# A fused attention and two-MLP kernel: 64-row transposes made with 128 rows, x sums on VectorE, g loaded first, and new plan offsets

## The chip, the cores and the metric

The program runs on one core of a Trainium2 chip. Its time is the device time of one execution in microseconds. Five engines work side by side from their own queues, each in program order: TensorE (PE, with its weight loads as PEld), VectorE (DVE), ScalarE (ACT), GpSimd (POOL) and SyncE (SP), which here issues all loads and stores.

## What is computed

In float32, with 4 batches, 12 heads, 448 tokens and a head size of 64:

```python
q_n, k_n = rmsnorm(q, g_q), rmsnorm(k, g_k)
scores = q_n @ k_n.T / 8            # per batch and head
attn = exp(scores - max); attn = attn / (sum + 1e-9)
x = concat_heads(attn @ v)          # 1792 x 768
x = ((x @ w_a) * (x @ w_b)) @ w_out         # inner width 1536
h = x @ w_in                                # inner width 2048
return (h * clip(h + 3, 0, 6) / 6) @ moe2_w_out
```

## The kernel before

**Precision.** Most products run as fp32r matmuls. An operand is split into a high half, rounded to fp32r, and a low half, the difference; a product is then three matmuls: high by high, high by low, low by high (`tri`, L694 to L696). Scores take two (L529, L530), with q split alone. Transposes of probabilities and the value product run in plain fp32.

**Tiling.** x lives transposed: six row tiles (m) of 128 features by 448 tokens for each batch. The first group is batches 0 and 1, the second batches 2 and 3. Attention goes head pair by head pair (`pair`, 24 of them). A pair has 896 tokens in seven chunks of 128, of which the fourth holds 64 rows of each head. `turn_k` transposes K for each head on TensorE (four transposes into one PSUM bank, L494). For the first head the fourth of them takes only the lower 64 rows of its chunk. After the scores come row maximum (L535), exponential (L539) and the transposes of the probabilities: `turn_p` for three full column blocks (L568), `turn_rest` for the last 64 columns of each head. `turn_rest` makes four 128x128 transposes (L582), three that give 64x128 (L584) and one of 64x64 rows (L585) that reads only the lower half of the shared chunk. `value` (L600) multiplies by v.

**The MLPs.** The first MLP runs first for batch 0, then batch 1, and the second MLP for both (`layer`), while attention for batches 2 and 3 is done in between. The last part (`layer7`, matmuls at L967) does both MLPs for the second group with a seven-product scheme for 2x2 blocks (as Strassen's). It needs sums and differences of blocks of x. `x_maker` makes them: `minus` (the sums, at `sub`, L393), a ScalarE copy for the high half (L711, L871) and a subtraction for the low half. Its subtractions may run on VectorE or GpSimd. For the first MLP of the second group they are made from `xf`, at the end of `layer(1, ...)`; for the second MLP from `acc`. In `layer7` the sums of weights are at L925, the splits of weights also at L393, and the accumulations of products from PSUM into `acc` or `xf` at L975. The accumulations of `layer` are at L800.

**The order of the work.** One core's queues are filled by a planner (`Plan`). Each operation is added with a due time, and with a cost in nanoseconds for each engine that may run it. `Plan.run` goes through a model of the five engines, and whenever one is free it issues the operation that is ready and due first; a second engine takes an operation if the first is busy and the due time is past by some margin (`LB`, `LF`). The order in which this loop calls the operations is the order of each engine's instructions, fixed for the run. The tables T, TQ, R, OA to OD, LEAD, OW, AFTER, MM, LW7, XLEAD and so on are due offsets, margins and costs of that model. `vg` and `"VG"` say which engines may run a subtraction: V is VectorE, G GpSimd.

**The start.** `gg` is the product of g_q and g_k, from a 1 KB load (L1100); the high half of q is q times gg (L511 on ScalarE, L513 on VectorE), the low half is at L517. The load was due at 0.0, behind the first pair's loads, which are due before 0. The squares for the norms are at L453 (ScalarE) or L455 (VectorE, GpSimd).

Of the kernel before, what the change touches and what calls it, by code (L numbers as in the profile page):

```python
# [18 lines left out]
P = 128  # L19
NB, NH, S, D = 4, 12, 448, 64  # L20
# [7 lines left out]

T = (6.793, 74.014, 253.235, 440.0)
TQ = (1.436, 3.637, 4.788, 4.218)
R = ((85.0, 1.761), (255.0, 1.223), (411.278, 1.34), (703.581, 1.0), (932.169, 1.0))


BS = ((2, 3, 4), (1, 2, 3, 4), (2, 3, 4), (3, 4))
# [7 lines left out]
SQ = ("AG", "A", "A", "A")  # L44
# [10 lines left out]

LB = ((344.344, 276.261, 381.127), (548.658, 402.965, 561.206), (548.658, 402.965, 561.206), (606.623, 311.013, 561.206))
LF = ((548.658, 376.129, 761.141), (548.658, 402.965, 561.206), (548.658, 402.965, 561.206), (553.891, -149.766, 668.974))
LW = 161.162  # L60


OA = (-7.027, -5.631, -5.6, -5.311, -5.026, -4.8, -4.475, -4.381)
OB = (-4.77, -2.7, -3.245, -2.3, -2.091, -2.6, -2.386)
OC = (0.104, -0.677, 0.482, 0.457, 4.632, 4.519)
UT = 5.13
UK = 2.0
OD = (0.4, 1.972, 3.0)


LEAD = 22.604
OW = (-8.493, -9.23, 1.129, 3.002, -1.61)
AFTER = 2.346


SLICE = (3, 3, 2)
# [3 lines left out]

MM = 206.7
LW7 = (26.748, 25.0, 15.217, 11.821)

SLICE7 = ((3, 3), (3, 3, 2))
XLEAD, XSTEP = -11.077, 4.422
LX7 = (10.733, 19.0, 18.5)  # L90


def piece_order(up, down, n, k):
# [214 lines left out]
def on_pool(n):  # L308
    return ((146 + 2.11 * n) * (1.25 if n >= PH else 1.0), True)
# [3 lines left out]
def fused_kernel(ctx: ExitStack, tc: tile.TileContext, nat, qt, gs_in, wpk, outT):  # L313
    nc = tc.nc
    V, A, G, SP = nc.vector, nc.scalar, nc.gpsimd, nc.sync
# [74 lines left out]
    add = plan.add  # L390
# [23 lines left out]
    def pair(n0):  # L414
# [8 lines left out]
        def at(u):  # L423
            return t0 + q * u
# [22 lines left out]
        for i, (lo, hi, who) in enumerate(alike):  # L447
# [3 lines left out]
            def square(e, sl=sl):  # L451
# [3 lines left out]
                    e.tensor_tensor(out=sq.t[:, sl], in0=rn.t[:, sl], in1=rn.t[:, sl], op=ALU.mult)  # L455

            cost = {"V": (on_dve(n), True), "A": on_act(n), "G": on_pool(n)}
            add(at(OA[0]), {k: cost[k] for k in ("VAA"[i] if n0 == 0 else SQ[b])}, square,
                reads=x, writes=sk)
            add(at(OA[1]), {"V": on_dve(n)}, lambda e, sl=sl: e.reduce_sum(out=ms.t[:, sl], in_=sq.t[:, sl], axis=AX.X),  # L460
                reads=sk, writes=m)
# [14 lines left out]
        for i in range(2):  # L476
# [15 lines left out]
            def turn_k(e, i=i, tk=tk):  # L492
                def turn(c, rows, at):
                    e.transpose(tk.t.bitcast(F32R)[:, at:at + rows.stop], kc.t[rows, c].rearrange("p a d -> p (a d)"),  # L494
                                identr[rows, rows])
                everyone = slice(0, P)
                if i == 0:
                    turn(3, lower, 3 * P)
                else:
                    turn(3, everyone, 2 * P + D)  # L500
                for c in range(3):
                    turn(4 * i + c, everyone, c * P)

            add(at(OB[3] + 4 * i), {"PE": 224 + 30 * i}, turn_k, writes=[tk, kks[i]], reads=[
                "identr", *((kc, k, a) for k in range(i + 1) for a in range(2))])
            add(at(OB[4] + 4 * i), {"A": 424}, lambda e, i=i, tk=tk: e.activation(kks[i].t, tk.t[:, :S], AF.Copy),
                reads=[tk], writes=[kks[i]])
# [51 lines left out]
        for k in range(4):  # L559
# [17 lines left out]
            else:  # L577
                t = bank("t", BT[b], False)

                def turn_rest(e, t=t):  # L580
                    for c in range(4):
                        e.transpose(t.t[:, c * P:(c + 1) * P], ps[3 + c].t[:, S - P:], ident)  # L582
                    for c in range(3):
                        e.transpose(t.t[lower, c * P:(c + 1) * P], ps[c].t[:, S - D:], ident)  # L584
                    e.transpose(t.t[lower, 3 * P:S], ps[3].t[lower, S - D:], ident[lower, lower])  # L585

                add(at(u), {"PE": 820}, turn_rest, reads=["ident", *ps], writes=[t, (pt, 0)])
                cost = copy_ps(4 * P)
                add(at(u + OD[0]), {x: cost[x] for x in PT[b]}, lambda e, t=t, pt=pt: copy(
                    e, pt.t[:, :4 * P], t.t), reads=[t], writes=[(pt, 0)])  # L590
# [9 lines left out]
                        e.matmul(pv.t[rows, :S], rv.t[own[i], at_v[i]], pt.t[own[i], cols[i]:cols[i] + S],  # L600
                                 start=k == 0, stop=k == 3)

            add(at(u + OD[1]), {"PE": 1750}, value, reads=[rv, *((t[1], x) for t in pts for x in range(2))], writes=[pv])
            pts = []
        m, due = h // 2, at(u + OD[2])
        if LATE[b]:
# [100 lines left out]
    def split(due, to, src, keys, out, gv, after=()):  # L707

        hi, lo = to
        vg = {"V": (535, True), "G": on_pool(S)}  # L710
        add(due, {"A": 467}, lambda e: e.activation(hi, src, AF.Copy), reads=keys, writes=out[:1], after=after)  # L711
        add(due + 1, {k: vg[k] for k in gv}, lambda e: sub(e, lo, src, f32(hi)),
            reads=[*keys, out[0]], writes=out[1:])
# [115 lines left out]
    def x_maker(src, key, base, after=(), holds=None):  # L829
# [4 lines left out]
        def came(mb, due):  # L834
# [4 lines left out]
            def hold(*those):  # L839
                return [] if holds is None else [holds[n * GB + i] for n, i in those]  # L840

            def at(name):
                return base + XLEAD + XSTEP * ("b11", "t1", "b22", "b21", "t2", "t3", "t4").index(name) + 0.6 * j

            def own(name, m, bi):
                hi, lo = xx[:, m, bi, 0], xx[:, m, bi, 1]
                out = parts(m, bi, ("xh", "xl"))
                split(at(name), (hi, lo), src[:, m, bi], [key(m, bi), *hold((m, bi))], out, "VG")
                sevens[name, j] = (lambda: (hi, lo)), out

            if bi == 0 or m >= HX:
# [2 lines left out]
            if not there.issuperset(all4):  # L854
                return
            (k11, k12, k21, k22), (x11, x12, x21, x22) = zip(*((key(*x), src[:, x[0], x[1]]) for x in all4))
            vg = {"V": (535, True), "G": on_pool(S)}

            def minus(name, out, x, y, reads, writes):
                add(at(name) - 0.5, vg, lambda e: sub(e, out, x, y), reads=reads, writes=writes, after=after)  # L860
# [236 lines left out]

    tails, stored, ends = [], set(), []
    A.preload_act_table_set("natural_log_exp_and_others")
    add(0.0, {"SP": 100}, lambda e: e.dma_start(out=gg, in_=gs_in), writes=["gg"])  # L1100
    add(0.0, {"G": 1500}, lambda e: make_identity(nc, ident), writes=["ident"])
    add(0.1, {"V": 200}, lambda e: e.memset(half_c, 0.5), writes=["half"])
    add(0.1, {"V": 200}, lambda e: e.tensor_copy(identr, ident), reads=["ident"], writes=["identr"])
# [80 lines left out]
```

## Time and profile before

| what | us |
|---|---|
| median of 3 runs | 1257.12 |
| lowest, highest | 1255.7, 1262.59 |
| span of the profiled execution | 1254.4 |
| TensorE busy | 1228.4 |
| VectorE busy | 1031.7 |
| ScalarE busy | 673.3 |
| GpSimd busy | 197.5 |

The time of the profiled execution is one of the runs above; its span, from the first to the last instruction, is 1.3 us below the lowest of them. Busy times are unions of overlapping instructions. Matmuls overlap, so what one costs is read from its start to the start of the next, not from its duration. Idle time is named with what ended it.

### The profile page before, as it was taken

Reading aid. Unit: us, or ns where it says so; the run is one execution under the profiler, and the core shown is the slowest. Engines: PE = TensorE matmul, PEld = TensorE weight load, DVE = VectorE, ACT = ScalarE, POOL = GpSimd, SP = SyncE. Lnnn points to the kernel's source line nnn. Section 1 sums busy time; section 2 is a strip of 40 time slices with the busy share of each in tenths; the row PEclk is TensorE's granted clock in tenths of the full one; section 3 lists DMA queues with packets and bytes.
Section 4 is the critical chain, followed back from the end, with each engine's and each line's share of the span. In section 5 each row is a group of like instructions: output and inputs, shape, how many; then the busy total and the mean of one; then the engine's idle time right before and its main releaser. Section 6 shows DMA issues by size and latency. Waiting matters only on the chain.

```text
span 1254.4 us, 18336 instructions
## 1 busy us (share of the span) xinstructions
PE 1228.4 (98%) x6342; PEld 1046.4 (83%) x6342; DVE 1031.7 (82%) x1906; ACT 673.3 (54%) x1422; POOL 197.5 (16%) x240
## 2 busy tenths in 40 slices
PE   5999999999999999999999999899999999999998
PEld 3678787878988888888788788799999998899998
DVE  7998999997557699888777765796977799988978
ACT  6998776665235545665666664332422245634433
POOL 2433232223011023010121100410000013000000
PEclk9999999999999999999999999899999999999999
DMA  6455766766686587656546442465364544455433
GB/s 203 164 174 186 243 223 228 248 227 230 242 296 241 182 287 272 219 185 227 208 143 207 172 157 77 144 215 161 110 200 143 162 148 129 151 175 165 139 101 126
DMA packets 107853, 235.57 MB, mean 188 GB/s; under 512 B 9200, under 2 KB 74096, under 8 KB 107760
## 3 DMA queue, kind: packets, MB, share of 16 engines
q1 hardware_dynamic: 107760, 234.39, 55.7%
q8 instruction: 50, 0.82, 0.3%
q14 instruction: 43, 0.35, 0.1%
HBM read 162.01 MB, written 72.35 MB: 187 GB/s over the span
## 4 chain that ended last, share of the span: by engine, by line
PE 84%; DVE 9%; DMA 3%; ACT 2%; issue 1%; SPq 0%; DVEq 0%; POOL 0%; ACTq 0%
PE bank L967 30%; PE bank L694 12%; PE bank L696 11%; PE bank L695 11%; PE bank L600 6%; PE bank L568 4%; PE bank L529 3%; PE bank L530 3%; DMA wst<-in_w_dram 2%; PE bank L494 1%; DVE act L393 1%; DVE acc L975 1%; PE bank L582 1%; DVE wf L655 1%; DVE w L393 1%
## 5 line engine op out<-in xcount | busy, mean ns | idle before, releaser
L694 PE MATMUL bank<-xx,w 128*128 128x448 f32 x480 | 184.0, 383 | 1.2 <-ACT p L539 1.1
L696 PE MATMUL bank<-xx,w 128*128 128x448 f32 x480 | 175.7, 366 | 0.0
L695 PE MATMUL bank<-xx,w 128*128 128x448 f32 x480 | 175.5, 366 | 0.0
L967 PE MATMUL bank<-act,w 128*128 128x448 f32 x711 | 153.2, 365 | 0.0
L967 PEld LDWEIGHTS bank<-act,w 128*128 128x128 f32 x711 | 133.5, 188 | 10.6
L694 PE MATMUL bank<-act,w 128*128 128x448 f32 x336 | 130.1, 387 | 4.1 <-DVE acc L800 4.1
L967 PE MATMUL bank<-xx,w 128*128 128x448 f32 x612 | 131.8, 365 | 0.0
L676 ACT ACTIVATE w<-wf 128x768 fp32r<-128x768 f32 x104 | 85.9, 842 | 83.0 <-PE bank L695 53.3
L696 PE MATMUL bank<-act,w 128*128 128x448 f32 x336 | 124.3, 370 | 0.0
L695 PE MATMUL bank<-act,w 128*128 128x448 f32 x336 | 124.2, 370 | 0.0
L967 PEld LDWEIGHTS bank<-xx,w 128*128 128x128 f32 x612 | 114.8, 188 | 9.4
L393 POOL TENSOR_TENSOR w<-wf,w 128x384 fp32r<-128x384 f32 x75 | 81.5, 1099 | 254.8 <-ACT w L676 240.3
L535 DVE TENSOR_REDUCE nm<-bank 128x1 f32<-128x448 f32 x168 | 102.4, 618 | 21.4 <-PE bank L530 18.0
L800 DVE TENSOR_TENSOR acc<-bank,acc 128x448 f32<-128x448 f32 x120 | 74.3, 620 | 51.3 <-PE bank L696 50.7
L404 ACT ACTIVATE pt<-bank 128x512 f32<-128x512 f32 (+1 forms) x131 | 70.8, 549 | 69.4 <-PE bank L568 64.4
L539 ACT ACTIVATE p<-bank,nm,rstd 128x448 f32<-128x448 f32 x132 | 95.2, 724 | 23.0 <-PE bank L584 11.5
L694 PEld LDWEIGHTS bank<-xx,w 128*128 128x128 f32 x480 | 90.2, 188 | 18.9 <-issue 7.8
L393 DVE TENSOR_TENSOR w<-wf,w 128x384 fp32r<-128x384 f32 x158 | 87.4, 587 | 13.4 <-ACT w L676 10.7
L696 PEld LDWEIGHTS bank<-xx,w 128*128 128x128 f32 x480 | 90.1, 188 | 7.9
L695 PEld LDWEIGHTS bank<-xx,w 128*128 128x128 f32 x480 | 90.4, 188 | 6.2
L967 PE MATMUL bank<-xt,w 128*128 128x448 f32 x405 | 88.6, 366 | 0.7 <-ACT xf L404 0.7
L600 PE MATMUL bank<-pt,rv 128*64 128x448 f32 (+1 forms) x384 | 86.2, 557 | 0.0
(192 smaller groups left out, 2431.1 us busy)
## 6 DMA issues: line engine op xcount, KB each, us to landing
wst<-in_w_dram SPq DMA_DIRECT2D x68, 768.0 KB, 5.7
split<-w SPq DMA_DIRECT2D x102, 384.0 KB, 3.6
w<-split SPq DMA_DIRECT2D x82, 384.0 KB, 3.7
kept<-wf SPq DMA_DIRECT2D x68, 384.0 KB, 2.8
wf<-kept SPq DMA_DIRECT2D x65, 384.0 KB, 4.2
wst<-kept SPq DMA_DIRECT2D x39, 384.0 KB, 3.6
rq<-in_qt_dram SPq DMA_DIRECT2D x48, 224.0 KB, 3.3
rn<-in_nat_dram SPq DMA_DIRECT2D x23, 448.0 KB, 4.2
```

Of the source, the lines that this page charges most:

```text
L393: e.tensor_tensor(out=out, in0=a, in1=b, op=ALU.subtract)
L404: A.activation(out, in_, AF.Copy)
L535: add(at(u + OC[1]), {"V": 531}, lambda e, s=s, nm=nm: e.tensor_reduce(out=nm.t, in_=s.t[:, :S], axis=AX.X, op=ALU.max, negate=True), read ...
L539: add(at(u + OC[3]), {"A": 704}, lambda e, j=j, s=s, nm=nm, p=p: e.activation(p.t, s.t[:, :S], AF.Exp, bias=nm.t, scale=rstd.t[:, qcol[j]: ...
L568: e.transpose(t.t[:, c * P:(c + 1) * P], ps[4 * i + c].t[:, k * P:(k + 1) * P], ident)
L600: e.matmul(pv.t[rows, :S], rv.t[own[i], at_v[i]], pt.t[own[i], cols[i]:cols[i] + S], start=k == 0, stop=k == 3)
L676: add(due - LEAD + OW[2], {"A": on_act(DM)}, lambda e: e.activation(w.t[:, 0], wf.t.bitcast(F32), AF.Copy), reads=both, writes=[(w, 0, 0), ...
L694: e.matmul(ps, w.t[:, 0, wsl], xh, start=start, stop=False)
L695: e.matmul(ps, w.t[:, 0, wsl], xl, start=False, stop=False)
L696: e.matmul(ps, w.t[:, 1, wsl], xh, start=False, stop=stop)
L800: add(due, {"V": 535}, lambda e, m=m, bi=bi, ps=ps: e.tensor_tensor(out=acc[:, m, bi], in0=ps.t[:, :S], in1=acc[:, m, bi], op=ALU.add), re ...
L967: e.matmul(out, w.t[:, a, chunk(c)], x, start=first and j + k == 0, stop=j + k == n + 1, skip_group_check=not first)
```

## The change

It does four things.

- `turn_k` makes the fourth transpose of the first head with all 128 rows and 128 columns, and `turn_rest` makes the fourth 64-column transpose with all 128 rows. The results that are read stay the same; the extra columns are not read.
- The subtractions in `x_maker` may run on VectorE alone. The second pair's square is done by ScalarE alone.
- The load of g is due at -1000, ahead of all others.
- The planner's due offsets, margins and costs are new, among them MM from 206.7 to 204.0.

```diff
-T = (6.793, 74.014, 253.235, 440.0)
+T = (6.793, 74.014, 255.311, 440.588)
...
-OA = (-7.027, -5.631, -5.6, -5.311, -5.026, -4.8, -4.475, -4.381)
+OA = (-7.027, -5.8, -5.6, -2.393, -5.026, -4.8, -4.475, -4.381)
...
-            add(at(OA[0]), {k: cost[k] for k in ("VAA"[i] if n0 == 0 else SQ[b])}, square,
+            add(at(OA[0]), {k: cost[k] for k in ("VAA"[i] if n0 == 0 else "A" if n0 == 2 else SQ[b])}, square,
...
                 if i == 0:
-                    turn(3, lower, 3 * P)
+                    turn(3, everyone, 3 * P)
...
-            add(at(OB[3] + 4 * i), {"PE": 224 + 30 * i}, turn_k, writes=[tk, kks[i]], reads=[
+            add(at(OB[3] + 4 * i), {"PE": 340}, turn_k, writes=[tk, kks[i]], reads=[
...
-                    for c in range(3):
+                    for c in range(4):
                         e.transpose(t.t[lower, c * P:(c + 1) * P], ps[c].t[:, S - D:], ident)
-                    e.transpose(t.t[lower, 3 * P:S], ps[3].t[lower, S - D:], ident[lower, lower])
...
-            add(at(u + OD[1]), {"PE": 1750}, value, reads=[rv, *((t[1], x) for t in pts for x in range(2))], writes=[pv])
+            add(at(u + OD[1]), {"PE": 1860}, value, reads=[rv, *((t[1], x) for t in pts for x in range(2))], writes=[pv])
...
-                split(at(name), (hi, lo), src[:, m, bi], [key(m, bi), *hold((m, bi))], out, "VG")
+                split(at(name), (hi, lo), src[:, m, bi], [key(m, bi), *hold((m, bi))], out, "V")
...
-            vg = {"V": (535, True), "G": on_pool(S)}
+            vg = {"V": (535, True)}
...
-    add(0.0, {"SP": 100}, lambda e: e.dma_start(out=gg, in_=gs_in), writes=["gg"])
+    add(-1000.0, {"SP": 100}, lambda e: e.dma_start(out=gg, in_=gs_in), writes=["gg"])
```

Since the planner lays all instructions out anew, three places of the resulting order follow. In the rows of the change, line numbers above L453 and below L586 are one higher than before, and so is the helper at L393.

TensorE, the turning of the last columns of one pair in the stage where attention and MLP matmuls alternate. Before:

```order
L696 MATMUL bank_64<-act_243,w_237 128x448
L582 MATMUL bank_68<-ident,p_269 128x128
L582 MATMUL bank_68<-ident,p_270 128x128
L582 MATMUL bank_68<-ident,p_271 128x128
L582 MATMUL bank_68<-ident,p_272 128x128
L584 MATMUL bank_68<-ident,p_266 64x128
L584 MATMUL bank_68<-ident,p_267 64x128
L584 MATMUL bank_68<-ident,p_268 64x128
L585 MATMUL bank_68<-ident,p_269 64x64
L694 MATMUL bank_70<-act_241,w_239 128x448
L695 MATMUL bank_70<-act_241,w_239 128x448
L696 MATMUL bank_70<-act_241,w_239 128x448
```

With the change, the same place:

```order
L696 MATMUL bank_64<-act_243,w_237 128x448
L583 MATMUL bank_68<-ident,p_269 128x128
L583 MATMUL bank_68<-ident,p_270 128x128
L583 MATMUL bank_68<-ident,p_271 128x128
L583 MATMUL bank_68<-ident,p_272 128x128
L585 MATMUL bank_68<-ident,p_266 64x128
L585 MATMUL bank_68<-ident,p_267 64x128
L585 MATMUL bank_68<-ident,p_268 64x128
L585 MATMUL bank_68<-ident,p_269 64x128
L694 MATMUL bank_70<-act_241,w_239 128x448
L695 MATMUL bank_70<-act_241,w_239 128x448
L696 MATMUL bank_70<-act_241,w_239 128x448
```

The 64x64 row is gone, and a fourth 64x128 row stands in its place; nothing else differs here.

VectorE, from the last value product of attention (copied out of bank_70) on, where the second MLP of the first group ends and the seven-product part begins. L925 are sums of weights, L800 accumulations that set banks 63, 64 and 70 free. Before:

```order
L408 COPY xf<-bank_70 128x448
L925 TENSOR_TENSOR ws_6861<-wst_232 128x384
L925 TENSOR_TENSOR ws_6862<-wst_233 128x384
L925 TENSOR_TENSOR wst_232<-wf_235,wst_232 128x384
L925 TENSOR_TENSOR wst_233<-wst_232,wst_233 128x384
L925 TENSOR_TENSOR wf_235<-ws_6861,wf_235 128x384
L925 TENSOR_TENSOR wst_232<-ws_6862,wst_232 128x384
L800 TENSOR_TENSOR acc<-bank_64,acc 128x448
L767 SCALAR_TENSOR_TENSOR bank_63<-tmp_247,bank_63 128x448
L800 TENSOR_TENSOR acc<-bank_70,acc 128x448
L393 TENSOR_TENSOR act_242<-bank_63,act_242 128x448
L800 TENSOR_TENSOR acc<-bank_64,acc 128x448
```

With the change:

```order
L409 COPY xf<-bank_70 128x448
L925 TENSOR_TENSOR ws_6861<-wst_232 128x384
L925 TENSOR_TENSOR ws_6862<-wst_233 128x384
L925 TENSOR_TENSOR wst_232<-wf_235,wst_232 128x384
L925 TENSOR_TENSOR wst_233<-wst_232,wst_233 128x384
L925 TENSOR_TENSOR wf_235<-ws_6861,wf_235 128x384
L767 SCALAR_TENSOR_TENSOR bank_63<-tmp_247,bank_63 128x448
L800 TENSOR_TENSOR acc<-bank_64,acc 128x448
L925 TENSOR_TENSOR wst_232<-ws_6862,wst_232 128x384
L394 TENSOR_TENSOR act_242<-bank_63,act_242 128x448
L800 TENSOR_TENSOR acc<-bank_70,acc 128x448
L394 TENSOR_TENSOR wb_6859<-ws_6861,wb_6859 128x384
```

Two accumulations stand later by one weight sum, and the next ones have single short instructions between them instead of standing in pairs; the sums of x follow in the same manner further on.

ScalarE, at the start. rn_252 holds the first pair's q and k, rn_253 the second pair's; kc is the split K, kk the turned one. Before:

```order
L453 ACTIVATE sq_258<-rn_252 128x256
L464 ACTIVATE rstd_216<-ms_214 128x4 x2
L466 ACTIVATE rstd_216<-rstd_216 128x4 x2
L453 ACTIVATE sq_258<-rn_252 128x384
L404 ACTIVATE kc_259<-rn_252 128x4x64
L511 ACTIVATE qh_260<-rq_254,gg 128x448
L464 ACTIVATE rstd_216<-ms_214 128x6
L466 ACTIVATE rstd_216<-rstd_216 128x6
L506 ACTIVATE kk_264<-bank_63 128x448
L511 ACTIVATE qh_261<-rq_255,gg 128x448
```

With the change:

```order
L454 ACTIVATE sq_258<-rn_252 128x256
L512 ACTIVATE qh_260<-rq_254,gg 128x448
L465 ACTIVATE rstd_216<-ms_214 128x4 x2
L467 ACTIVATE rstd_216<-rstd_216 128x4 x2
L454 ACTIVATE sq_258<-rn_252 128x384
L454 ACTIVATE sq_258<-rn_253 128x896
L465 ACTIVATE rstd_216<-ms_214 128x6
L467 ACTIVATE rstd_216<-rstd_216 128x6
L405 ACTIVATE kc_259<-rn_252 128x4x64
L465 ACTIVATE rstd_217<-ms_215 128x14
L467 ACTIVATE rstd_217<-rstd_217 128x14
L405 ACTIVATE kc_259<-rn_252 128x3x64
```

The high half of q comes second, and the square of rn_253, the Ln and Exp behind it and then the high half of K follow in this order; before, the high half of K stood right behind the first pair's squares.

## Rows read from the trace of the kernel before

**Rows 1.** The page, busy time: engine, us, share of the span, instructions.

```profile
PE 1228.4 (98%) x6342; PEld 1046.4 (83%) x6342; DVE 1031.7 (82%) x1906; ACT 673.3 (54%) x1422; POOL 197.5 (16%) x240
```

**Rows 2.** Windows: stretch, its length, busy us (count) of PE, PEld, DVE, ACT, POOL, clock, DMA.

```profile
50.00:85.00 35.00, 35.00 (x243) 23.90 (x243) 31.48 (x64) 34.05 (x90) 15.40 (x28) 1.00 0.51 168
...
785.00:815.00 30.00, 25.91 (x109) 21.41 (x108) 22.59 (x33) 9.23 (x19) 15.18 (x12) 0.89 0.40 143
1025.00:1085.00 60.00, 58.13 (x283) 52.46 (x283) 58.88 (x103) 34.59 (x68) 14.49 (x11) 1.00 0.51 165
```

**Rows 3.** Timeline, PE at a turn_rest: start us, length us, line, op, names, count, [idle].

```profile
417.25 0.60 PE L582 MATMUL bank<-ident,p 128*128 128x128 f32 x4
417.68 0.49 PE L584 MATMUL bank<-ident,p 128*64 128x128 f32 x3
418.11 0.24 PE L585 MATMUL bank<-ident,p 64*64 64x64 f32 x1
...
418.59 0.36 PE L695 MATMUL bank<-act,w 128*128 128x448 f32 x1
```

**Rows 4.** Timeline, PE at four plain transposes of turn_p.

```profile
441.99 0.60 PE L568 MATMUL bank<-ident,p 128*128 128x128 f32 x4
...
442.63 0.36 PE L695 MATMUL bank<-xx,w 128*128 128x448 f32 x1
442.83 0.37 PE L696 MATMUL bank<-xx,w 128*128 128x448 f32 x1
```

**Rows 5.** Timeline, PE at two turn_k groups, of a first and of a second head.

```profile
464.00 0.37 PE L530 MATMUL bank<-kk,ql 128*128 128x448 f32 x1
464.30 0.63 PE L494 MATMUL bank<-identr,kc 64*128 64x64 f32 x4
...
465.04 0.36 PE L530 MATMUL bank<-kk,ql 128*128 128x448 f32 x1
...
473.80 0.37 PE L696 MATMUL bank<-xx,w 128*128 128x448 f32 x1
...
474.58 0.36 PE L695 MATMUL bank<-xx,w 128*128 128x448 f32 x1
```

**Rows 6.** Timeline, PE: its two long waits, and the pace behind the second.

```profile
795.62 0.47 PE L694 MATMUL bank<-act,w 128*128 128x448 f32 x1 [1.82 <-DVE acc L800]
...
805.84 0.47 PE L694 MATMUL bank<-act,w 128*128 128x448 f32 x1 [2.26 <-DVE acc L800]
...
806.90 0.57 PE L695 MATMUL bank<-act,w 128*128 128x448 f32 x1
807.27 0.57 PE L696 MATMUL bank<-act,w 128*128 128x448 f32 x1
```

**Rows 7.** Windows behind the two waits; the clock is the seventh number.

```profile
796.00:800.00 4.00, 4.00 (x14) 3.60 (x13) 1.97 (x5) 1.94 (x4) 2.78 (x3) 0.57 0.46 172
...
806.00:810.20 4.20, 4.20 (x14) 3.74 (x15) 1.55 (x4) 0.52 (x1) 0.26 (x1) 0.59 0.55 196
```

**Rows 8.** Timeline, POOL and DVE at the first of the waits.

```profile
789.18 4.03 POOL L393 TENSOR_TENSOR xf<-xf 128x448 f32<-128x448 f32 x3
...
789.32 2.87 DVE L925 TENSOR_TENSOR ws<-wst 128x384 f32<-128x384 f32 x2
...
793.55 0.54 DVE L925 TENSOR_TENSOR wst<-wst,wst 128x384 f32<-128x384 f32 x1
```

**Rows 9.** Timeline, DVE beside two GpSimd subtractions at 1045.57 to 1048.54.

```profile
1046.02 1.50 DVE L925 TENSOR_TENSOR wst<-wf,wst 128x384 f32<-128x384 f32 x1
```

**Rows 10.** Chain and timeline at the start: g, first turning, GpSimd square, third pair.

```profile
3.07 4.10 DMA gg<-in_g_dram
...
8.26 0.87 PE L494 MATMUL bank<-identr,kc 64*128 64x64 f32 x4 [8.26 <-DVE kc L393]
...
9.36 1.70 POOL L455 TENSOR_TENSOR sq<-rn 128x896 f32<-128x896 f32 x1 [8.06 <-DVE nt L470]
...
35.22 0.73 ACT L539 ACTIVATE p<-bank,nm,rstd 128x448 f32<-128x448 f32 x1
```

More of the change, by code (lines that the diff above doesn't have):

```diff
@@ L26 @@
 PH = DM // 2
-T = (6.793, 74.014, 253.235, 440.0)
-TQ = (1.436, 3.637, 4.788, 4.218)
-R = ((85.0, 1.761), (255.0, 1.223), (411.278, 1.34), (703.581, 1.0), (932.169, 1.0))
+T = (6.793, 74.014, 255.311, 440.588)
+TQ = (1.436, 3.632, 4.787, 4.218)
+R = ((85.0, 1.761), (255.0, 1.223), (411.278, 1.34), (703.581, 1.035), (932.169, 0.974))
 BS = ((2, 3, 4), (1, 2, 3, 4), (2, 3, 4), (3, 4))
@@ L54 @@
 LATE = (True, False, False, False)
-LB = ((344.344, 276.261, 381.127), (548.658, 402.965, 561.206), (548.658, 402.965, 561.206), (606.623, 311.013, 561.206))
-LF = ((548.658, 376.129, 761.141), (548.658, 402.965, 561.206), (548.658, 402.965, 561.206), (553.891, -149.766, 668.974))
-LW = 161.162
-OA = (-7.027, -5.631, -5.6, -5.311, -5.026, -4.8, -4.475, -4.381)
[L64 to L73, printed above, removed]
+LB = ((337.33, 254.341, 423.192), (544.511, 382.64, 561.206), (548.658, 402.965, 512.134), (606.623, 245.797, 550.397))
+LF = ((644.102, 328.928, 909.676), (561.504, 402.965, 561.206), (544.479, 420.172, 734.353), (553.891, -176.273, 668.974))
+LW = 378.341
+OA = (-7.027, -5.8, -5.6, -2.393, -5.026, -4.8, -4.475, -4.381)
+OB = (-4.77, -2.609, -3.245, -2.3, -2.045, -3.972, -1.906)
+OC = (0.063, -0.823, 0.674, 0.457, 4.597, 3.684)
+UT = 5.111
+UK = 1.966
+OD = (0.385, 1.995, 2.971)
+LEAD = 24.776
+OW = (-8.776, -11.002, 1.129, 7.735, -1.106)
+AFTER = -1.638
 SLICE = (3, 3, 2)
 XORDER = [(m, bi) for j in range(NX // 2) for bi in range(GB) for m in (j, j + NX // 2)]
-MM = 206.7
-LW7 = (26.748, 25.0, 15.217, 11.821)
+MM = 204.0
+LW7 = (12.37, 15.958, 16.974, 12.916)
 SLICE7 = ((3, 3), (3, 3, 2))
-XLEAD, XSTEP = -11.077, 4.422
-LX7 = (10.733, 19.0, 18.5)
+XLEAD = -11.759
+XSTEP = 4.11
+LX7 = (9.546, 15.358, 20.075)
 def piece_order(up, down, n, k):
@@ L582, in turn_rest @@
                         e.transpose(t.t[:, c * P:(c + 1) * P], ps[3 + c].t[:, S - P:], ident)
-                    for c in range(3):
+                    for c in range(4):
                         e.transpose(t.t[lower, c * P:(c + 1) * P], ps[c].t[:, S - D:], ident)
-                    e.transpose(t.t[lower, 3 * P:S], ps[3].t[lower, S - D:], ident[lower, lower])
-                add(at(u), {"PE": 820}, turn_rest, reads=["ident", *ps], writes=[t, (pt, 0)])
+                add(at(u), {"PE": 880}, turn_rest, reads=["ident", *ps], writes=[t, (pt, 0)])
                 cost = copy_ps(4 * P)
```

## The prediction

> **What bounds the kernel now.** I read the page's busy times first: TensorE is busy 1228.4 of 1254.4 us [rows 1]. The reader is to see that only two things can shorten this kernel: fewer TensorE nanoseconds, or the 26 us in which it stands still. Then the windows, to see where another engine is as full: ScalarE is busy 34.05 of 35 us at 50 to 85 us, VectorE 58.88 of 60 us at 1025 to 1085 [rows 2]. There, time saved on TensorE can be held up by the other engine, and work added to that engine can cost. Then TensorE's timeline at a single turning, to read prices from start to start, since its durations overlap. Last the timelines of VectorE and GpSimd at the longest waits.
>
> **The turnings of the rest (L582 to L585).** From the start of the first transpose to the start of the second matmul behind the group, eight transposes take 417.25 to 418.59 = 1.34 us [rows 3]. The four 128x128 ones take 0.43 us of it to the start of the 128x64 ones at 417.68, and those three take another 0.43 to the start of the 64x64 one at 418.11, so a stall stands ahead of that one. The same measure over four plain transposes is 441.99 to 442.63 = 0.64 us, and the next matmul starts 0.20 later [rows 4]. Eight plain ones are then 0.43 + 0.64 = 1.07, if the 128x64 form leaves as freely as it is entered (it is entered at the plain pace [rows 3]). Saved: 0.27 us for each of 24 pairs, 6.5 us. Below, it could leave at the price at which a change to 64 rows is entered, some 0.1 us: 0.17 x 24 = 4.1.
>
> **The turnings of K (L494).** With a 64-row one at the head, from the start of the matmul ahead to the start of the second matmul behind: 464.00 to 465.04 = 1.04 us. The group of four 128-row ones: 473.80 to 474.58 = 0.78 [rows 5]. Saved: 0.26 us, 24 times, 6.2 us; a few of these groups stand right behind the value matmuls, where the two forms differ by only 0.1, so I take 5.8. Both together: 12.3 us, all of it on TensorE's own queue. In both cases it is the change of form that costs, not the number of columns.
>
> Here a rule speaks against the change. The Trainium skill, TensorEngine Tiling (Array Packing), Overview, promises up to 2x for operands of 64 or fewer, since small tiles work independently. By that rule the 64-row form should be the cheaper one and the change a small loss. The same page's Tiling Modes says that a change of tiling mode drains the array; the trace shows this second effect as the larger [rows 3, 5].
>
> Six of the 24 pairs lie in the first 85 us, where ScalarE has about 3% of slack [rows 2]. I count half of their 3.1 us, so the turnings bring 12.3 - 1.5 = 10.8. Ends: 9.1 x 18/24 = 6.8 (dear exit, nothing in the first stage) and 12.3.
>
> **The x sums, first place (785 to 815 us).** TensorE waits 1.82 and 2.26 us for an accumulation on VectorE [rows 6], and after each wait the granted clock falls: 0.57 over 4 us and 0.59 over 4.2 us [rows 7], that is half clock for 2 x 3.44 us. Matmuls start 0.37 us apart there [rows 6] instead of 0.20 [rows 4], so 6.9 x (1 - 0.20/0.37) = 3.1 us more. Together 7.2 us. The cause is in the next timeline: while GpSimd subtracts, VectorE instructions with two SBUF inputs take 2.87 us for two, against 0.54 for the same line without it [rows 8]. So GpSimd does not help VectorE here, it blocks it. The change takes 12 such GpSimd instructions out of this stretch [rows 2]; VectorE gets 12 x 0.54 = 6.5 us more and loses six stretches of (2.87 - 2 x 0.54)/2 = 0.9, 5.4 us (the first two of the six stand in [rows 8]). That is 1.1 us more work in a stretch in which VectorE was busy 22.6 of 30. The new order also puts each accumulation at most three short instructions (1.6 us) behind the last, while TensorE needs 1.2 us per product and has three banks. Following the new order with 0.54 per instruction, the accumulations keep ahead of the banks and neither wait remains. I take 7.2 - 1.1 = 6.1. Ends: 0 (the waits only move) and 7.2.
>
> The Trainium skill, SBUF - State Buffer, section SBUF: two separate sides, says that the shared pair is an exclusive lock and that the loser fully blocks; by that rule each moved subtraction frees its whole GpSimd time, some 1.3 us. The trace agrees in kind, with about 0.9 each.
>
> **The x sums, second place (1025 to 1085 us).** VectorE is full, and GpSimd runs 11 instructions there [rows 2]. They come to VectorE, 11 x 0.54 = 5.9 us; a stretched one reads 1.50 [rows 9] against 0.54 [rows 8], and six of those (with a few smaller) are 6 us. Even: 0. Ends: TensorE's 1.87 us of idle in this stretch [rows 2] go, or 3 us come on top.
>
> **g first, and the start.** g was issued at 3.07 and landed 4.10 us later [rows 10]; the q products waited for it. Now it goes ahead, and the five loads that it passes move back one issue of 0.47 us. But in the new order ScalarE also does the second pair's square ahead of the first pair's normalisation, and that data is there only at about 9.2 us: GpSimd started on it at 9.36 in the old order, and g, issued just before it, came at 7.17. From there the square, Ln, Exp and the two halves of K take some 2.5 us (an estimate from the durations of these steps in the old start), so the first turning starts near 11.7 instead of 8.26 [rows 10]. Against that, nothing then waits for q, and GpSimd's square of 1.70 us, beside which VectorE stretched, is gone. I followed ScalarE's new order with the durations in the trace: the third pair's first exponential, at 35.22 before [rows 10], comes at 35.5, and with 0.7 for waits at 36.2. Cost 1.0. Ends: -1 and +4.
>
> **The rest of the plan.** The order of TensorE keeps its shape: the same 6102 matmul rows, nearly the same number of changes between turnings, values and products, and filler products that begin some 2 us earlier. SP issues the same loads in nearly the same order. GpSimd loses 59 instructions, VectorE gets 51 and ScalarE 8, over the whole run. I cost this at 0, covered by the idle shares of VectorE and ScalarE; if the cover is gone at one place, a wait of the kind in [rows 6] costs 2 us and 1.5 us of clock. Ends: -2 and +5.
>
> **Sum.** -10.8 - 6.1 + 0 + 1.0 + 0 = -15.9. The profiled span is 1254.4, the runs are 1255.7 to 1262.6 with a median of 1257.1, so 1 to 3 us lie around the span. Span 1238.5, time **1241.2 us**.
>
> **Rivals.**
> *A, the waits only move* (10%): the turnings bring 10.8, but at the first place VectorE, now with all the sums, is late somewhere else by as much. For it: VectorE has more to do there than before. Against: the stretches go. Time 1257.1 - 10.8 + 1.0 = 1247.3.
> *B, the small tiles were the cheap ones* (4%): no switch is saved, and 48 instructions of twice the columns get longer by at most half the plain pace of 0.43/4, 48 x 0.054 = 2.6 us; with the other terms 1257.1 + 2.6 - 6.1 + 1.0 = 1254.6. Against it: [rows 3, 5]. The tiling page's Overview, named above, is what speaks for it.
> *C, VectorE becomes the bound* (5%): place 1025 to 1085, and on to the end. It decides if the stretches there were mostly on time that VectorE had to spare: then 5.9 us of work come to a full engine, and because the new offsets put sums ahead of accumulations, each late accumulation costs TensorE about 2 us plus 1.5 of clock, as in [rows 6, 7]. Six or more such waits are 21 us, and with the start at +4: 1257.1 - 10.8 + 21 + 4 - 6.1 = 1265.2. Slower than before.
> *D, the start is the dear part* (8%): +4 there and nothing from the first six pairs' turnings: 1241.2 + 3 + 1.5 = 1245.7.
> *Forecast* (73%).
>
> **How the numbers follow.** The range takes the forecast's ends: all gains, 12.3 + 7.2 + 1.9 + 1 + 2 = 24 less, some 1233; dear exits, 4 us at the start and one or two new waits: about 1252. It holds A and D. Range 1232 to 1252. A measurement of this kernel tells about 0.5%, 6.3 us, from no change, so faster means below 1250.8: forecast, A and D nearly whole, with some of the new-wait cases taken off, 0.84; the same, 0.11 (B, part of A and of the waits); slower, above 1263.4, 0.05 (C).
>
> **What would show it.** TensorE without any 64x64 turning, eight transposes and the next two matmuls in about 1.07 us, K groups in 0.78; no waits of 2 us and clock 1.00 at about 780 to 805; GpSimd empty there; the first turning at 11 to 12 us and the third pair's first exponential within 2 us of 35; a span of some 1238. I am wrong if a 128x64 transpose is left with a stall, if TensorE's total of waits stays at 26 us, or if VectorE's busy share passes 99% over a longer stretch than 60 us.

## The result, and the profile after

The kernel after takes 1243.01 us (median of 4 runs, 1240.69 to 1244.8), the kernel before 1259.32 (4 runs, three of them those above): a ratio of 0.988, 95% interval 0.985 to 0.991. The forecast was 1241.2 in a range of 1232 to 1252. The profiled span is 1239.0 us, where 1238.5 was forecast. The total came out, but not all of its parts did.

The page of the kernel after, busy time, answers [rows 1]: TensorE is busy 13.8 us less for the same 6342 matmuls, and still 98% of the span.

```profile
PE 1214.6 (98%) x6342; PEld 1041.7 (84%) x6342; DVE 1038.3 (84%) x1957; ACT 673.0 (54%) x1430; POOL 150.7 (12%) x181
```

TensorE's timeline at the turning of [rows 3], and at a turning of K for a first head as in [rows 5]:

```profile
417.40 0.60 PE L583 MATMUL bank<-ident,p 128*128 128x128 f32 x4
417.84 0.60 PE L585 MATMUL bank<-ident,p 128*64 128x128 f32 x4
418.19 0.45 PE L694 MATMUL bank<-act,w 128*128 128x448 f32 x1
418.48 0.36 PE L695 MATMUL bank<-act,w 128*128 128x448 f32 x1
...
461.94 0.37 PE L531 MATMUL bank<-kk,ql 128*128 128x448 f32 x1
462.15 0.46 PE L495 MATMUL bank<-identr,kc 128*128 128x128 f32 x4
462.44 0.43 PE L530 MATMUL bank<-kk,qh 128*128 128x448 f32 x1
462.72 0.37 PE L531 MATMUL bank<-kk,ql 128*128 128x448 f32 x1
```

Read as before: 417.40 to 418.48 is 1.08 us where it was 1.34, and 461.94 to 462.72 is 0.78 where it was 1.04. The group leaves the 128x64 form at the plain pace.

The windows of [rows 2] in the kernel after (length, then busy us and count of PE, PEld, DVE, ACT, POOL, then the clock, DMA):

```profile
50.00:85.00 35.00, 35.00 (x240) 23.61 (x236) 33.56 (x72) 33.58 (x88) 8.37 (x18) 1.00 0.66 216
...
785.00:815.00 30.00, 30.00 (x149) 27.80 (x148) 29.46 (x58) 12.44 (x25) 0.00 (x0) 1.00 0.65 219
...
1025.00:1085.00 60.00, 59.11 (x291) 54.13 (x290) 60.00 (x117) 37.72 (x75) 0.00 (x0) 1.00 0.47 145
```

At 785 to 815 TensorE is busy throughout at full clock (149 matmuls, 109 before), GpSimd is empty, and VectorE is at 29.46 of 30 us. At 1025 to 1085 VectorE is full, and yet TensorE stands still less than before (0.89 us, 1.87 before).

Of the signs that were to show the prediction wrong, one came. VectorE is over 99% busy for a stretch of 110 us, where more than 60 was to be the sign:

```profile
980.50:1090.50 110.00, 109.11 (x537) 100.24 (x536) 109.33 (x212) 59.64 (x118) 0.00 (x0) 1.00 0.46 141
```

TensorE is idle for 0.89 us of it, so the sign was badly chosen: a full engine is not yet one that is waited for. TensorE's idle time, the second sign, is 24.4 us of the span against 26.0, only just below: the two waits of [rows 6] are gone, but 3.5 us more pass ahead of the first turning.

The start, from the timelines of SP, ScalarE and TensorE, answers [rows 10]:

```profile
0.74 0.39 SPq L1100 DMA_DIRECT2D gg<-in_g_dram  x1
...
9.25 0.95 ACT L454 ACTIVATE sq<-rn 128x896 f32<-128x896 f32 x1 [1.24 <-DMA rn<-in_nat_dram]
...
11.78 0.75 PE L495 MATMUL bank<-identr,kc 128*128 128x128 f32 x4 [11.78 <-DVE kc L394]
```

ScalarE does wait for the second pair's data until 9.25, and the first turning starts at 11.78 (forecast 11.7).

Where the time went is read best at equal work. TensorE does the same kinds of work in both kernels, 48 value products among them (groups of L600), and in the timelines the same value products stand at the same count of instructions. Start of each in us:

| TensorE starts | before | after | difference |
|---|---|---|---|
| 1st value product (59th matmul) | 29.90 | 29.60 | -0.30 |
| 4th | 49.96 | 49.62 | -0.34 |
| 13th | 126.86 | 127.42 | +0.56 |
| 22nd | 258.22 | 258.41 | +0.19 |
| 48th, the last | 786.86 | 780.67 | -6.19 |
| first product of the last part (L967) | 813.65 | 799.60 | -14.05 |
| last matmul | 1250.51 | 1235.04 | -15.47 |

So in the first 258 us, with the probabilities of 11 pairs turned, nothing was won. That was not forecast, and most of the experiments are about it. "At the nth value product" below means such a comparison of two profiles. One profile is one execution; how far two of the same order lie apart is said at run 12.

### The profile page after: what moved, and what is told of

It reads as the page before. It is cut to its first block, busy times and chain, and to the rows that moved or that the text cites. A ratio compares the mean times of both kernels' runs of the same rounds, so it can differ in the third digit from the quotient of the medians.

```text
span 1239.0 us, 18325 instructions
## 1 busy us (share of the span) xinstructions
PE 1214.6 (98%) x6342; PEld 1041.7 (84%) x6342; DVE 1038.3 (84%) x1957; ACT 673.0 (54%) x1430; POOL 150.7 (12%) x181
## 4 chain that ended last, share of the span: by engine, by line
PE 81%; DVE 10%; DMA 5%; ACT 3%; issue 1%; SPq 0%; DVEq 0%; ACTq 0%
PE bank L967 34%; PE bank L694 11%; PE bank L696 10%; PE bank L695 10%; PE bank L600 5%; PE bank L569 3%; DMA wst<-in_w_dram 3%; PE bank L530 3%; PE bank L531 2%; DMA rn<-in_nat_dram 1%; DVE wf L655 1%; DVE wf L652 1%; DVE nm L536 1%; DVE w L394 1%; DVE wf L649 1%
## 5 line engine op out<-in xcount | busy, mean ns | idle before, releaser
L967 PE MATMUL bank<-act,w 128*128 128x448 f32 x729 | 156.2, 365 | 0.0
L967 PEld LDWEIGHTS bank<-act,w 128*128 128x128 f32 x729 | 136.9, 188 | 10.9
L394 POOL TENSOR_TENSOR w<-wf,w 128x384 fp32r<-128x384 f32 x81 | 93.4, 1167 | 326.0 <-ACT w L676 297.3
L967 PE MATMUL bank<-xx,w 128*128 128x448 f32 x585 | 126.3, 365 | 0.0
L967 PEld LDWEIGHTS bank<-xx,w 128*128 128x128 f32 x585 | 109.7, 188 | 9.0 <-DVE acc L975 0.2
L800 DVE TENSOR_TENSOR acc<-bank,acc 128x448 f32<-128x448 f32 x120 | 74.6, 622 | 47.2 <-PE bank L696 46.7
L694 PEld LDWEIGHTS bank<-xx,w 128*128 128x128 f32 x480 | 90.2, 188 | 18.1 <-issue 8.5
L405 ACT ACTIVATE pt<-bank 128x384 f32<-128x384 f32 (+1 forms) x125 | 67.8, 546 | 62.7 <-PE bank L569 58.1
L696 PEld LDWEIGHTS bank<-xx,w 128*128 128x128 f32 x480 | 90.1, 188 | 7.9
L695 PEld LDWEIGHTS bank<-xx,w 128*128 128x128 f32 x480 | 90.5, 188 | 6.0
L967 PE MATMUL bank<-xt,w 128*128 128x448 f32 x414 | 90.6, 365 | 0.7 <-ACT tmpx L405 0.7
L600 PE MATMUL bank<-pt,rv 128*64 128x448 f32 (+1 forms) x384 | 86.2, 557 | 0.0
```

The source lines that it names most:

```text
L394: e.tensor_tensor(out=out, in0=a, in1=b, op=ALU.subtract)
L405: A.activation(out, in_, AF.Copy)
L694: e.matmul(ps, w.t[:, 0, wsl], xh, start=start, stop=False)
L695: e.matmul(ps, w.t[:, 0, wsl], xl, start=False, stop=False)
L696: e.matmul(ps, w.t[:, 1, wsl], xh, start=False, stop=stop)
L800: add(due, {"V": 535}, lambda e, m=m, bi=bi, ps=ps: e.tensor_tensor(out=acc[:, m, bi], in0=ps.t[:, :S], in1=acc[:, m, bi], op=ALU.add), re ...
```

## The experiments

All were timed in 5 rounds against the kernel before on the same chip. Intervals are 95%.

**1. The turnings alone.** In the kernel before, only this (planner costs kept, so no other instruction moves):

```diff
-                    turn(3, lower, 3 * P)
+                    turn(3, everyone, 3 * P)
...
-                    for c in range(3):
+                    for c in range(4):
                         e.transpose(t.t[lower, c * P:(c + 1) * P], ps[c].t[:, S - D:], ident)
-                    e.transpose(t.t[lower, 3 * P:S], ps[3].t[lower, S - D:], ident[lower, lower])
```

> The kernel before, with nothing changed but the 128-row turnings (the planner's costs for them are left, so every other instruction keeps its place on every engine). Theory 1, the change of form costs and TensorE's own queue sets the time everywhere: 24 x (0.27 + 0.26) = 12.7 us less, the gain growing evenly from pair to pair. Theory 2, in the first 255 us another engine sets the pace, as a comparison of the two profiles suggests (the kernel after has done the same number of TensorE instructions 0.2 us later at 258 us): only the last 12 pairs gain, 6.4 us less, whatever the plan. Rival B, small tiles are the cheap ones: 2.6 us more.

Measured: 0.9934 (0.9921 to 0.9948), 8.3 us less. Profile against before: -1.8 us at the 4th value product, -3.2 at the 13th, -3.5 at the 22nd, -10.5 at the last. The gain is there before 255 us too, where theory 2 allows none, and rival B has the wrong sign: both fall. The total of 8.3 us lies between the two theories all the same. This profile gives back 4.2 us in the last part, by its pace there (last section); how many of the other executions did so is not known. Behind the last value product this profile shows what the x sums are about, unchanged by the turnings:

```profile
785.11 0.47 PE L694 MATMUL bank<-act,w 128*128 128x448 f32 x1 [1.83 <-DVE acc L800]
...
794.25 0.47 PE L694 MATMUL bank<-act,w 128*128 128x448 f32 x1 [2.79 <-DVE acc L800]
```

**2. The same undone in the kernel after.** The same edit backwards.

> The kernel after, with the 64-row turnings put back and nothing else (same order on every engine). Theory 1, TensorE's queue sets the time everywhere: 12.7 us slower than the kernel after, about the time of before less 3 us. Theory 2, in the first 255 us another engine sets the pace: 6.4 us slower than the kernel after, about 10 us faster than before. Rival B: 2.6 us faster than the kernel after.

Measured: 1.0018 (1.0008 to 1.0028) of before, that is 16 to 18 us slower than the kernel after (0.988, and 0.989 in run 12). In the profiles the loss against after grows evenly: 1.0 us at the 4th value product, 2.1 at the 13th, 4.6 at the 22nd, 13.6 at the last. Some 5 us more come from the pace of the last part (last section). So in the order of after, too, the turnings bring most of what they are priced at in the first 258 us (4.6 of some 6 us); they are not swallowed by ScalarE. It follows that something else in the change loses them again there: with the old turnings the new order is 4.8 us behind before at the 22nd value product.

**3. The x sums alone.** In the kernel before:

```diff
-..., out, "VG")
+..., out, "V")
-            vg = {"V": (535, True), "G": on_pool(S)}
+            vg = {"V": (535, True)}
```

> The kernel before, with the x sums on VectorE alone and nothing else; the planner lays the queues out anew from there on with its old offsets. If GpSimd's subtractions blocked VectorE: the waits of 1.82 and 2.26 us and the clock of 0.57 to 0.59 behind them go, 6 to 9 us less. If the waits only move (rival A): no waits of GpSimd's making but others of the same sum, within 2 us of before. If VectorE becomes the bound at 1025 to 1085 us (rival C): 5 us more or worse there.

Measured: 0.9944 (0.9932 to 0.9956), 7.0 us less. Between the last value product and the last part 26.79 us become 19.07. Its windows:

```profile
785.00:815.00 30.00, 30.00 (x147) 26.02 (x147) 28.61 (x57) 12.83 (x25) 0.00 (x0) 1.00 0.64 220
1025.00:1085.00 60.00, 57.66 (x283) 52.48 (x282) 59.99 (x118) 35.46 (x70) 0.00 (x0) 1.00 0.48 151
```

No wait and full clock in the first place, with the old offsets; rival A falls. In the second place TensorE is idle 2.34 us instead of 1.87: 0 within half a microsecond, so rival C falls too, but nothing is won there.

**4. The x sums on both engines in the kernel after.** The same edit backwards.

> The kernel after, with the x sums allowed on GpSimd again and nothing else. If GpSimd's subtractions blocked VectorE: 6 to 9 us slower than the kernel after, with waits of some 2 us on an accumulation and a lower granted clock at 780 to 805 us. If the new offsets alone cured the waits: within 2 us of the kernel after.

Measured: 0.9947 (0.9933 to 0.9961) of before, some 7 to 9 us slower than the kernel after (see run 2). The waits are back, with the new offsets. GpSimd, VectorE and TensorE in their timelines:

```profile
783.70 4.03 POOL L394 TENSOR_TENSOR xf<-xf 128x448 f32<-128x448 f32 x3
...
783.84 2.87 DVE L925 TENSOR_TENSOR ws<-wst 128x384 f32<-128x384 f32 x2
786.63 1.51 DVE L925 TENSOR_TENSOR wst<-wf,wst 128x384 f32<-128x384 f32 x1
788.06 0.55 DVE L925 TENSOR_TENSOR wst<-wst,wst 128x384 f32<-128x384 f32 x1
...
790.20 0.47 PE L694 MATMUL bank<-act,w 128*128 128x448 f32 x1 [1.89 <-DVE acc L800]
...
801.28 0.47 PE L694 MATMUL bank<-act,w 128*128 128x448 f32 x1 [1.09 <-DVE acc L800]
```

The pair of 2.87 us of [rows 8] stands there to the hundredth, beside the same three GpSimd subtractions of 4.03 us, and 0.55 as soon as they are over. This stretch is 3.5 us longer than in after. The lower clock that was expected does not come: it stays at 1.00 behind these two waits. Another 2.1 us are lost in the last part, some 1.8 of them by its pace (last section), and 0.7 before this stretch.

**5. Both parts together.** Edits 1 and 3 in the kernel before, nothing else.

> The kernel before with the 128-row turnings and the x sums on VectorE, g where it was and the old offsets. If the parts add up, the turnings' 10.5 us up to the last value product (787 us of before) and the x sums' 7.7 behind it come together: 18 us less than before, 2 to 3 us faster than the kernel after, and the remaining parts of the change (g first, new offsets) cost 4 us before 787 us and give 2 behind it. If the new offsets are needed for the gains to meet: 15 us less than before at most, no faster than the kernel after.

Measured: 1236.1 us, 0.9848 (0.9828 to 0.9868), 19 us less. That is more than the 15 us of runs 1 and 3 together. In the profiles, where the pace can be left out, the parts add up: 10.5 us by the last value product (run 1) and 7.7 behind it (run 3), against 11.9 and 7.8 here, within the spread of single profiles (run 12). Profile against before: -5.8 us at the 22nd value product, -11.9 at the last, -19.7 at the start of the last part, -19.0 at the end. This is the lowest median of all kernels here.

**6. g first alone.** In the kernel before, the load due at -1000 and the square of the second pair on ScalarE.

> The kernel before with g loaded first and the second pair's square on ScalarE, nothing else; ScalarE's order at the start becomes that of the kernel after up to the second pair's norm. Prediction's theory: first turning at 11 to 12 us instead of 8.26, and about 1.0 us lost by 50 us, nothing later. Rival, g first carries the loss that the kernel after shows up to 190 us: 4 us or more lost by then. Rival, g first is a gain: 1 us won by 50 us.

Measured: 1.0054 (1.0032 to 1.0076), 6.8 us slower. Profile against before: -0.4 us at the 59th matmul (in before the 1st value product; here that one stands ten matmuls later, at 30.35), +2.0 at the 4th value product, +5.7 at the 13th, +6.6 at the 17th, +5.4 at the last. The first turning is at 11.65, as forecast, but the cost comes later. TensorE's timeline has waits at places where before has none:

```profile
38.70 0.48 PE L530 MATMUL bank<-kk,ql 128*128 128x448 f32 x1 [0.66 <-DVE ql L517]
83.31 0.47 PE L529 MATMUL bank<-kk,qh 128*128 128x448 f32 x1 [0.32 <-ACT p L539]
91.77 0.44 PE L568 MATMUL bank<-ident,xf 128*128 128x128 f32 x2 [0.56 <-ACT xf L539]
99.34 0.53 PE L494 MATMUL bank<-identr,kc 128*128 128x128 f32 x4 [0.29 <-ACT pt L404]
```

From the 4th to the 13th value product TensorE needs 80.6 us instead of 76.9. Counted over its timeline there, 1.2 of the 3.7 us are idle (0.0 before). It also changes 85 times instead of 78 between kinds of work (turnings of K, scores, turnings of probabilities, turnings of sums, value products, MLP products). That such changes carry the other 2.5 us is worked out, at some 0.35 us each, and not shown by a run. In the kernel after the same stretch has 84 changes, 0.2 us of idle and 77.8 us, against 75.4 in the fifth run, which has the same turnings.

**7. The load of g ahead, in an unchanged order.** To the kernel of run 11 (below; the order of the fifth run up to the last value product) the load is added by hand ahead of the plan, and the plan's own operation does nothing:

```diff
-    add(0.0, {"SP": 100}, lambda e: e.dma_start(out=gg, in_=gs_in), writes=["gg"])
+    add(0.0, {"SP": 100}, lambda e: None, writes=["gg"])
...
     with tc.manual_schedule():
+        SP.dma_start(out=gg, in_=gs_in)
```

> The kernel with the parts and the late offsets, with the load of g put ahead of all other loads by hand: every other instruction keeps its place on every engine, five loads are issued one step of 0.47 us later. If the load itself is the dear part of g first: 1 us or more lost by the first value product, 4 or more by 190 us. If the planner's reaction is the dear part: between 1.5 us won (the wait of 0.8 to 1.3 us for the low half of q goes) and 0.5 lost, all in the first 30 us and nothing later.

Measured: 0.9868 (0.9845 to 0.9892), against 0.9883 (0.9858 to 0.9907) of run 11 on the same chip: no difference that can be told. The start in TensorE's timeline:

```profile
9.13 0.75 PE L494 MATMUL bank<-identr,kc 128*128 128x128 f32 x4 [9.13 <-DVE kc L393]
11.61 0.74 PE L529 MATMUL bank<-kk,qh 128*128 128x448 f32 x1 [1.73 <-ACT kk L506]
12.37 0.74 PE L530 MATMUL bank<-kk,ql 128*128 128x448 f32 x1
```

The wait for the low half of q is gone, but the turning is 0.8 to 1.2 us later and the first product waits for the turned K instead. At the 1st value product it is 0.7 us behind run 11, at the 22nd 1.4 ahead. So it is not the load itself that costs 5 us in the sixth run, but the order that the planner makes with it (there the square is fixed to ScalarE as well).

**8. g at its old place in the kernel after.**

> The kernel after with g loaded where it was before; the planner lays all queues out anew. If g first is what costs in the kernel after too: 4 to 5 us faster, won by 190 us. If the new attention offsets have already absorbed it: within 2 us of the kernel after.

Measured: 0.9919 (0.99 to 0.9939), some 3 to 5 us slower than the kernel after, where 4 to 5 faster was expected. Both theories fall. This order loses elsewhere in the first stage: at the 13th value product it is 2.8 us behind before in spite of its turnings, with waits of up to 1.09 us on VectorE:

```profile
51.82 0.47 PE L530 MATMUL bank<-kk,qh 128*128 128x448 f32 x1 [1.09 <-DVE pt L409]
74.89 0.47 PE L530 MATMUL bank<-kk,qh 128*128 128x448 f32 x1 [0.45 <-DVE pt L409]
```

g first is thus not bad in itself either. Each order that the planner made anew for the first 190 us was worse than the one of before. At the 17th value product, against the order of before with the same turnings (run 5, for run 6 the kernel before), after is 5.2 us behind, run 6 6.6 and this one 7.5.

**9 and 10. Old offsets in the kernel after.** In run 9 OA, OB, OC, OD, UT and UK of before, in run 10 LEAD, OW and AFTER.

> The kernel after with the attention's due offsets (OA, OB, OC, OD, UT, UK) of before; everything else as after. If these offsets carry the 5 us that the new order loses before 787 us: 4 to 5 us faster than the kernel after, won between 50 and 190 us. If not: within 2 us of the kernel after.

> The kernel after with the weights' due offsets and the products' lag (LEAD, OW, AFTER) of before; everything else as after. If these carry the loss of the new order before 787 us: 4 to 5 us faster than the kernel after. If they are what keeps VectorE ahead of the accumulations: 2 to 5 us slower, with waits on an accumulation. If neither: within 2 us.

Measured: 0.9895 (0.9875 to 0.9915) and 0.9894 (0.9872 to 0.9916), both within some 2 us of the kernel after. Neither table alone carries the loss. The margins and costs (LB, LF, LW, MM, T and the costs of the turnings) were not put back by any run. The profile of run 9 is 5.5 us behind after at the last value product, but it is that of its slowest execution of six (1246.22, the others 1239.8 to 1243.6), so this is not taken as its cost. Its granted clock is also half for 3.4 us each at 69.7 and 151.6 us, which the profile of after has nowhere between 22 us and the end of TensorE's work.

**11. Both parts with the late offsets only.** Run 5, with the last two rates of R, LW7, XLEAD, XSTEP and LX7 of the change.

> The kernel before with the 128-row turnings, the x sums on VectorE, and of the new constants only those of the last part (the last two rates of R, LW7, XLEAD, XSTEP, LX7); g where it was, old attention and weight offsets. The order is that of the run with the two parts up to the last value product. Theory, the parts add up: 12 us by the last value product, 7.7 behind it, and 1.8 at 1025 to 1085 us, where the run with the two parts lost 0.5 instead: 21 us less than before, 5 less than the kernel after. Rival, the late offsets only fit the order of the kernel after: no better than the run with the two parts (19 us less than before).

Measured: 0.9883 (0.9858 to 0.9907), 1236.43 to 1245.83 us over six executions. In the second place the late offsets do their work: from the 5301st to the 5501st matmul, 1037 to 1080 us in before, TensorE needs 42.3 us, against 43.4 in before and 43.9 in run 5. But the profiled execution needed 8.3 us more by the pace of the last part, and the 21 us less were not reached: by its times this kernel is no faster than the kernel after (0.988 and, in run 12, 0.989), though its profile is 3.1 us ahead of it at the last value product. Whether 21 would be reached at the shorter pace stays open.

**12. The kernel after once more.**

> The kernel after, unchanged, as the measure for the versions above. If the run with the turnings and the x sums alone really is the better kernel: 0.988 of before here, 3 us behind that run's 0.985. If matmuls run at one of two paces (0.2026 or 0.2067 us from start to start) for long stretches, by chance of an execution: this profile's time from the start of the last part to its end differs from the first profile's by 0.0041 us times the products spent at the longer pace, up to 8 us, with the order the same; and up to the last value product the two profiles agree within 1.5 us.

Measured: 0.9891 (0.9871 to 0.9911). Run 5, at 0.9848, is 5 us better against the kernel before on its chip, and the two intervals do not overlap; on run 5's own chip runs 9 and 10, which are near the kernel after, took 1241.9 and 1242.4 us against 1236.1. Run 11, with the order of run 5 up to the last value product, does not show this difference in its times.

This profile and the first of after, with the same order, lie 0.9 us apart one way and 1.7 the other before the last value product, and 0.3 more in the last part, where both have the shorter pace. More profiles share an order up to the last value product. Its start in all of them, in us:

| | order of before | order of after |
|---|---|---|
| 64-row turnings | before 786.86, run 3 786.15 | run 2 794.26 |
| 128-row turnings | run 1 776.35, run 5 774.92, run 11 777.61 | after 780.67, run 4 781.38, run 12 782.37 |

The turnings bring 8.5 to 11.9 us in the old order and 11.9 to 13.6 in the new one; the new order loses 7.4 to 8.1 us with the old turnings and 3.1 to 7.5 with the new ones (means 776.3 and 781.5, 5.2 apart). Run 5's is the luckiest of its three profiles: at the 22nd value product runs 1 and 11 are 2.3 and 3.3 us behind it. Over 1 us of that is one wait for an exponential, at the same instruction in all three (run 5, run 1, run 11):

```profile
188.55 0.47 PE L529 MATMUL bank<-kk,qh 128*128 128x448 f32 x1 [0.19 <-ACT xf L539]
```

```profile
189.93 0.47 PE L529 MATMUL bank<-kk,qh 128*128 128x448 f32 x1 [1.35 <-ACT xf L539]
```

```profile
191.78 0.47 PE L529 MATMUL bank<-kk,qh 128*128 128x448 f32 x1 [1.65 <-ACT xf L539]
```

So a single profile of the first stage is good to some 3 us, and a loss of 5 us there is read from all of them.

## Why the prediction was right, and where it was not

*The turnings* (10.8, ends 6.8 and 12.3): right. The prices of 1.07 and 0.78 are in the rows, and by the last value product they are worth 8.5 to 11.9 us in the old order and 11.9 to 13.6 in the new one (run 12). Half of the first six pairs' gain was written off because ScalarE is full there [rows 2]; at the 9th value product (82 us in before) runs 1, 5 and 11 have 2.7, 2.9 and 1.6 of their 3.1 us, so half was a little low. Rival B is excluded by runs 1 and 2. The Trainium skill, TensorEngine Tiling (Array Packing), Tiling Modes, has the change of mode drain the array, and the traces agree with that where the rows change from 128 to 64 (0.27 and 0.26 us a group), not with the gain for small tiles that its Overview promises. For a change of columns alone they show no such price: four 128x64 transposes stand between the others in the group of 1.08 us, where eight plain ones were reckoned at 1.07.

*The x sums, first place* (6.1, ends 0 and 7.2): right in mechanism, too small. Runs 3 and 5 and the change itself win 7.7 to 7.9 us. The term that failed is "That is 1.1 us more work": VectorE's busy time rose to 28.61 of 30 us in run 3, and TensorE still never waited for it, so nothing had to be taken off. The rest is the clock, priced at 3.1 us. From the last value product to the last part TensorE's 94 matmuls are busy for 22.81 us before and 19.00 after, 3.8 less, and its 4.1 us of idle time are gone:

```profile
786.80:813.70 26.90, 22.81 (x94) 18.75 (x94) 20.32 (x28) 8.13 (x17) 15.18 (x12) 0.87 0.36 130
```

```profile
780.60:799.60 19.00, 19.00 (x94) 16.28 (x93) 18.47 (x36) 8.04 (x17) 0.00 (x0) 1.00 0.48 173
```

The trace agrees with what the Trainium skill says of the lock in SBUF - State Buffer, section SBUF: two separate sides: run 4 shows the stretched pair again. Rivals A and C are excluded by run 3: VectorE does fill up behind 980 us, as C has it, but TensorE does not wait for it.

*The second place* (0): the x sums did bring 0 (runs 3 and 5, within 0.5 us). That TensorE's time from the 5301st to the 5501st matmul still fell by 1.8 us (43.4 to 41.6) goes with the new offsets of the last part, which were costed at 0: the kernels with them need 0.3 to 1.9 us less there than before (six of nine 1.5 to 1.9), those without from 0.4 less to 0.5 more.

*The start* (1.0): if anything too dear. The first turning is at 11.78, as forecast. The row at 35.22 in [rows 10] that the prediction called the third pair's first exponential is the second pair's sixth. The third pair's first one stood at 37.72 in before; it is at 37.13, 36.08 and 36.19 in the three profiles of the new order (after, runs 4 and 12), and at 36.24, 35.99 and 36.33 in runs 1, 5 and 11, which have the same turnings and the old start. So the new start costs 1.1 us in one profile and nothing that can be told in the others. Rival D, the start as the dear part, falls with this: what it would look like, no gain in the first stage, did come, but from another place.

*The rest of the plan* (0, ends -2 and +5): this step failed. "The order of TensorE keeps its shape" held over the run (from the 17th value product on, 447 changes of kind in before and 435 in after; the 6102 matmul rows that the prediction names are 6342 in [rows 1]), but not in the first stage. The cover named, "the idle shares of VectorE and ScalarE", is thin there: VectorE is busy 31.48 and ScalarE 34.05 of 35 us at 50 to 85 in before [rows 2]. By the table of run 12 the new order is 3.1 to 7.5 us behind at the last value product, 5.2 by the means; less what the start costs, some 4 to 5 us are the rest's, at the very end of what was allowed for it.

So the forecast of -15.9 against a measured -15.5 on TensorE is right by errors that cancel, which is luck: 4 to 5 us lost in the order, against 1.7 more from the x sums, 1.8 more at the second place, up to 1 less for the start, and turnings that came out within a few us of their 10.8. What in the planner makes its new orders of the first stage worse was not settled: run 6 shows that moving g's load and the square is enough, run 8 that moving the load back is no cure, runs 9 and 10 that neither table alone is to blame, and the margins and costs were not tried.

## What to carry to other kernels

Price small pieces from the start of one instruction to the start of the next around them, in the trace: here a change of rows cost 0.26 to 0.27 us a group, more than the columns that the smaller form saves. Where two engines share a port, look for pairs of rows whose durations stretch together, and give the work to the engine that is waited for. When a heuristic planner's constants change with the code, test the code change in the old order by itself: here it was worth 19 us (run 5), and the whole change 14 to 16. And take more than one profile of an order before a difference of a few us is explained.

## What the runs showed of the hardware that was not expected

Matmuls of 128x448 that follow one another without a wait run at one of two paces, at a granted clock of 1.00 in both. From the timelines the starts repeat as 202, 203, 202, 199, 207 ns (mean 0.2026 us) or as 207, 207, 206 (0.2067). The pace holds for hundreds of products and in the rows looked at it changes where the row is broken by a stall or a slip of a few ns. The same window of the last part in runs 5 and 11, where the order is nearly the same:

```profile
850.00:1000.00 150.00, 150.00 (x742) 139.00 (x741) 118.48 (x222) 47.05 (x91) 0.00 (x0) 1.00 0.50 150
```

```profile
850.00:1000.00 150.00, 150.00 (x727) 136.26 (x726) 114.89 (x215) 45.63 (x88) 0.00 (x0) 1.00 0.50 149
```

742 matmuls in 150 us against 727. Over the 2142 products of the last part this is up to 8.8 us; run 11's profile had 8.3 of them, run 1's 4.9, and before and after nearly none. It is as large as several of the effects above, so the profiles were compared at equal work and stretch by stretch. What picks the pace was not tried.

The clock did not fall behind every wait of the same length: it was 0.57 behind the 1.82 us of [rows 6, 7], but stayed at 1.00 behind 1.83 us in run 1 and 1.89 us in run 4, and was 0.66 at 794 to 798 us around and behind 2.79 us in run 1. The 3.1 us counted for the clock are therefore not owed to the waits' length alone; what else decides was not tried.
